# A feed-forward stage with TensorE's order from the program and its scale factors taken in three separated steps

## The chip, the cores and the metric

The kernel runs on one core of a Trainium2 chip (trn2). The metric is the device time of one execution in microseconds (us), given as the median of several runs. Beside the runs stands one execution recorded by the hardware profiler; all rows below come from it.

## The reference

Three layers follow one another: causal attention with a decay, a dense feed-forward layer with a low-rank token mixing, and a layer of four experts of causal attention with a gate that takes two of four. The change lies in the second, which is

```python
batch, seq, d_model = (4, 576, 512)
xt = x.transpose(0, 2, 1)
h = xt @ U @ V                       # rank 32
u = x + h.transpose(0, 2, 1)
ch = np.maximum(u @ w_ch1, 0.0) @ w_ch2      # 512 -> 2048 -> 512
return (u + ch).astype(np.float32)
```

The weights arrive as 64-bit words and are narrowed to 32 bits on the chip.

## The kernel before, in words

**Precision by two parts.** Every large product is made of three: high by high, high by low, low by high. For the first half of the hidden features the parts are fp32r; for the second half they are f16, and there weights and u are first multiplied by a power of two that brings their largest value into range.

**Tiling.** The hidden features are split into four quarters q of 512 (NQ = 4, FT = 4 tiles of 128). A batch of u is held as [128, 4, 576] in DRAM (udram) and worked on in two halves c of 288 columns (HC = 288, NC = 2). The sum y goes to ydram between visits.

**Steps.** The list `steps` (L529 to L541) has 32 entries (batch b, half c, quarter q): 0 to 15 do quarters 0 and 1 (fp32r), 16 to 23 quarters 2 and 3 of batches 0 and 1, 24 to 31 quarters 2 and 3 of batches 2 and 3 (f16). QX0 = 14, QX1 = 16 and QX2 = 24 are places in it. `ffn_stream` (L554) yields after each group: a group of 12 matmuls for a hidden tile of the *next* step (`ffn_hidden`, L497) alternates with a group of 12 for an output tile of this step (`ffn_out`, L513), eight groups a step. The hidden tile is evicted by ScalarE (hh, L508) and then VectorE (hl, L509), the output by VectorE (L523, or L525 with the scale taken back). Both kinds share three PSUM buffers (psf).

**Before and beside it.** Up to the last pair of attention heads the groups fill TensorE's gaps in the attention. 79 groups are done that way. The rest, from step 9 on, is the dense stage alone, and the changed lines are there.

**Weights of quarters 2 and 3.** `narrow_quarter` (L399) reads eight raw tiles of 512 KB on the SP queue into two buffers, narrows each on ScalarE (L338, L340) and VectorE (L341, L342) and takes its maximum on VectorE (L419). `power` (L381) makes a factor of 128 maxima: TensorE turns them into a row (amt, L384), VectorE takes the maximum and keeps the exponent bits (L388 to L390), TensorE spreads it over the partitions by a product with ones (rsp, L393), VectorE makes the factor and its reciprocal (es, L395 and L396). `convert_quarter` (L432) then writes the f16 parts on ScalarE (L447) and VectorE (L448) into the buffers that quarter 0 (pool wx) or quarter 1 (pool wy) leaves free. The loop at L933 does this for quarter 2 about QX0 and for quarter 3 about QX1, with one 8-tile buffer (wfull).

**u in f16.** `ffn_load16` (L451) loads a half of u on the SP queue (L456), takes its maximum (uam, L458), calls `power`, scales on ScalarE (uhf, L462) and VectorE (ulf, L463) and loads the sum (L465). It is called 12 times, from `ffn_prepare` two steps ahead: once per half and quarter for batches 0 and 1, once per half for batches 2 and 3. Its buffers are a pool of six (fy2) for steps 14 to 23, a pool of three (fy) else. The fp32r steps use `ffn_load` (L478) with a low part made by GpSimd (ul, L490).

**What sets the order.** Each engine has its own queue and works through it in order. Under `tc.manual_schedule(engines={PE})` TensorE's queue has the order of the program; the attention before and after runs like that. Elsewhere, and on all other engines and the SP queue always, a planner orders the instructions: it plays the program through with estimated durations and lets an engine take the earliest instruction of the program that is ready by these. Before the change the dense stage's TensorE order is the planner's too. After the stage `load_y` (L974) and the lines from L955 on bring in the experts' weights and the first y; the planner may start them during the stage.

Of the kernel before, what the change touches and what calls it, by code (L numbers as in the profile page):

```python
# [8 lines left out]
F32 = mybir.dt.float32  # L9
# [9 lines left out]
P = 128  # L19
# [42 lines left out]
def kernel(  # L62
# [318 lines left out]
    def power(am):  # L381
# [10 lines left out]
        rp = ps1.tile([P, 1], F32, name="rsp", tag="av")  # L392
# [6 lines left out]
    def narrow_quarter(w32, q):  # L399
# [15 lines left out]
        for t in range(2 * FT):  # L415
            if t + 1 < 2 * FT:
                read(t + 1)
            narrow_bytes(w32[:, t, :], raws.pop(0)[:].rearrange("p (n two) -> p n two", two=2))
            nc.vector.tensor_reduce(am[:, t // FT, t % FT:t % FT + 1], w32[:, t, :], AX.X, OP.max,  # L419
                                    apply_absolute_value=True)  # L420
            yield
        sides = []
        for s in range(2):
            a1 = cur["s16"].tile([P, 1], F32, name="wa1", bufs=2)
            nc.vector.tensor_reduce(a1[:], am[:, s, :], AX.X, OP.max)
            sides.append(power(a1[:]))
            yield
        back = cur["s16"].tile([P, 1], F32, name="wback", bufs=2)
# [3 lines left out]
    def convert_quarter(wp, w32, q):  # L432

        shapes = [[P, KT, FT * P]] * 2 + [[P, FT, DM]] * 2
        w1h, w1l, w2h, w2l = [wp.tile(sh, F16, name=n + "f", tag=n)
                              for sh, n in zip(shapes, ("w1h", "w1l", "w2h", "w2l"))]
        W[q] = w1h, w1l, w2h, w2l
# [13 lines left out]
    def ffn_load16(b, c, fy):  # L451

        fu = cur["fu"]
        cs = slice(c * HC, c * HC + HC)
        ust = fy.tile([P, KT, HC], F32, name="ust", tag="yc")
        nc.sync.dma_start(ust[:], udram[b, :, :, cs])  # L456
        am = cur["s16"].tile([P, 1], F32, name="uam", bufs=2)
        nc.vector.tensor_reduce(am[:], ust[:], AX.XY, OP.max, apply_absolute_value=True)  # L458
        es = power(am[:])
        uh = fu.tile([P, KT, HC], F16, name="uhf", tag="uh")  # L460
        ul = fu.tile([P, KT, HC], F16, name="ulf", tag="ul")
        nc.scalar.mul(uh[:], ust[:], es[:, 1:2])  # L462
        nc.vector.scalar_tensor_tensor(ul[:], ust[:], es[:, 1:2], uh[:], OP.mult, OP.subtract)  # L463
        yc = fy.tile([P, KT, HC], F32, name="yc", tag="yc")
        nc.sync.dma_start(yc[:], ydram[b, :, :, cs])  # L465
        return uh, ul, yc, es
# [30 lines left out]
    def ffn_hidden(t, weights, uh, ul, dt=F32R):  # L497
# [5 lines left out]
        for n, (wa, xa, k) in enumerate(todo):  # L503
            nc.tensor.matmul(ph[:], wa[:, k, fs], xa[:, k, :], start=n == 0,  # L504
# [39 lines left out]
    def ffn_prepare(i):  # L544
        if i >= len(steps) or i in loads:
            return
# [807 lines left out]
```

## Time and profile before

| what | value |
|---|---|
| time, median of 3 runs | 909.58 us (905.0 to 912.32) |
| the profiled execution's own time | 904.65 us |
| its span, first to last instruction | 902.9 us, mean granted TensorE clock 0.966 |
| TensorE matmuls busy | 796.7 us (88%), 7428 |
| VectorE busy | 615.9 us (68%) |
| ScalarE busy | 432.6 us (48%) |
| GpSimd busy | 282.8 us (31%) |
| DMA | 101.95 MB, 113 GB/s in the mean |

How to read the rows: PE is TensorE, PEld its weight loads, DVE VectorE, ACT ScalarE, POOL GpSimd, SP the engine whose queue issues most transfers; a q behind a name is that engine's sequencer. Times are us from the span's start. The chain is the work that ended last, followed back from the last instruction, each time to what released it. In a table of stretches a row has the stretch, its length, each engine's busy time with its instructions in brackets, the granted clock of TensorE (1.00 is 2.4 GHz, 0.50 is 1.2), the busy share of the 16 DMA engines and GB/s. A group of instructions has the line, engine, operation, out<-in, count, busy us, mean ns of one, and behind the last bar the engine's idle time just before them with what ended it. A row of the timeline has start, duration, engine, line, operation, and in brackets the idle time before it and its releaser. A wait has its sum in us, how often, and the longest. A matmul's end is modelled, so that neighbours overlap and a short gap doesn't show as idle time.

### The profile page before, as it was taken

To read this page: it belongs to the slowest core of one execution; us is meant where nothing else is said; L and a number is where in the kernel's file an instruction comes from. 1 tells how busy PE (TensorE), PEld (TensorE's weight loads), DVE (VectorE), ACT (ScalarE), POOL (GpSimd) and SP (SyncE) were. 2 spreads that over 40 slices of the span, in tenths; PEclk is the share of its full clock that TensorE was granted. 3 is DMA by queue.
4 is the path that set the end of the run, shared out by engine and by line. 5 is a ranking of instruction groups with operands and counts; after the bars stand their busy time and mean duration, and the time that the engine had idled before them with its cause. 6 is when DMAs were issued, how large, how long until landed. Compare 5 with 4: busy or idle time off the path is not lost.

```text
span 902.9 us, 19107 instructions
## 1 busy us (share of the span) xinstructions
PE 796.7 (88%) x7428; PEld 714.6 (79%) x7428; DVE 615.9 (68%) x1626; ACT 432.6 (48%) x836; POOL 282.8 (31%) x367
## 2 busy tenths in 40 slices
PE   2787587889999989989998798996999999989997
PEld 2686577879999889988986576774677889889886
DVE  6999898966766676547568755434443578876775
ACT  4686665654555544434235321223211367675664
POOL 9856546543423341031110000006100734341210
PEclk9998699999999999999998899998999999999999
DMA  6345475542432432035377434224310422412122
GB/s 189 111 115 157 135 231 160 177 151 81 127 102 76 120 102 75 15 114 176 110 258 221 133 106 131 80 80 132 103 53 28 125 55 66 107 47 75 34 74 86
DMA packets 67370, 101.95 MB, mean 113 GB/s; under 512 B 5152, under 2 KB 48016, under 8 KB 67280
## 3 DMA queue, kind: packets, MB, share of 16 engines
q1 hardware_dynamic: 62720, 91.96, 34.6%
q10 hardware_dynamic: 4560, 8.78, 2.6%
q8 instruction: 58, 0.95, 0.4%
q14 instruction: 32, 0.26, 0.1%
HBM read 60.33 MB, written 22.56 MB: 92 GB/s over the span
## 4 chain that ended last, share of the span: by engine, by line
PE 52%; DVE 19%; DMA 16%; ACT 5%; issue 4%; POOL 3%; SPq 1%; DVEq 0%; POOLq 0%; ACTq 0%
PE cps L520 15%; PE hps L504 13%; PE sc L228 6%; DMA ust<-udram 5%; DMA raw<-in_w_dram 5%; DVE ph L244 4%; PE po L1154 3%; PE pv L1112 2%; PE pq L1047 2%; DVE ub L185 2%; PE ub L180 2%; PE gp L710 2%; PE av L259 1%; PE av L263 1%; PE av L261 1%
## 5 line engine op out<-in xcount | busy, mean ns | idle before, releaser
L244 DVE TENSOR_TENSOR ph<-pf,ph 128x576 f16<-128x576 f32 x144 | 128.1, 894 | 30.4 <-ACT ph L243 29.6
L508 ACT ACTIVATE hh<-hps 128x288 fp32r<-128x288 f32 (+1 forms) x128 | 52.1, 409 | 185.9 <-PE hps L504 177.1
L509 DVE SCALAR_TENSOR_TENSOR hl<-hps,hh 128x288 fp32r<-128x288 f32 (+1 forms) x128 | 57.7, 451 | 77.2 <-ACT hh L508 76.5
L238 ACT ACTIVATE pf<-sc 128x576 f32<-128x576 f32 x144 | 84.4, 613 | 36.8 <-PE sc L228 29.9
L243 ACT CAST ph<-pf 128x576 f16<-128x576 f32 x144 | 89.6, 637 | 9.7 <-POOL pf L240 8.2
L228 PE MATMUL sc<-qa,ka 128*128 128x288 f32 (+4 forms) x288 | 74.0, 317 | 18.0 <-DMA qa<-mr 6.4
L185 DVE CUSTOM_DVE_ANT_0 ub<-ub,maskm 128x448 f32<-128x448 f32 x192 | 81.6, 425 | 10.7 <-PE ub L180 8.7
L520 PE MATMUL cps<-hh,w2h 128*128 128x288 f32 x256 | 81.2, 317 | 2.3 <-DVE hl L509 2.0
L520 PE MATMUL cps<-hh,w2hf 128*128 128x288 f16 x256 | 74.3, 290 | 5.2 <-DVE hl L509 4.4
L520 PE MATMUL cps<-hh,w2l 128*128 128x288 f32 x256 | 77.2, 302 | 0.0
L520 PE MATMUL cps<-hl,w2h 128*128 128x288 f32 x256 | 77.0, 301 | 0.0
L259 PE MATMUL av<-vh,ph 128*128 128x65 f16 x720 | 74.5, 199 | 2.0 <-DVE x L308 2.0
L504 PE MATMUL hps<-uh,w1h 128*128 128x288 f32 x256 | 74.0, 311 | 2.3 <-DVE hl L509 2.3
L504 PE MATMUL hps<-uhf,w1hf 128*128 128x288 f16 x256 | 68.7, 297 | 7.4 <-ACT uhf L462 6.2
L520 PE MATMUL cps<-hl,w2hf 128*128 128x288 f16 x256 | 74.3, 290 | 0.0
L520 PE MATMUL cps<-hh,w2lf 128*128 128x288 f16 x256 | 74.3, 290 | 0.0
L261 PE MATMUL av<-vl,ph 128*128 128x64 f16 x720 | 74.0, 196 | 0.0
L263 PE MATMUL av<-vh,ph 128*128 128x65 f16 x720 | 73.7, 196 | 0.0
L259 PEld LDWEIGHTS <-ph 128*128 128x128 f16 x720 | 67.6, 100 | 6.1 <-DVE x L308 2.1
L504 PE MATMUL hps<-uh,w1l 128*128 128x288 f32 x256 | 70.6, 298 | 0.0
L228 PEld LDWEIGHTS sc<-qa,ka 128*128 128x128 f32 x288 | 51.8, 198 | 23.6 <-ACT pf L238 5.0
L504 PE MATMUL hps<-uhf,w1lf 128*128 128x288 f16 x256 | 68.6, 296 | 0.0
(221 smaller groups left out, 2391.7 us busy)
## 6 DMA issues: line engine op xcount, KB each, us to landing
raw<-in_w_dram SPq DMA_DIRECT2D x32, 512.0 KB
ust<-udram SPq DMA_DIRECT2D x20, 576.0 KB
qkt<-in_qk_dram SPq DMA_DIRECT2D x16, 576.0 KB
yc<-ydram SPq DMA_DIRECT2D x14, 576.0 KB
ydram<-yc SPq DMA_DIRECT2D x14, 576.0 KB
vr<-in_v_dram SPq DMA_DIRECT2D x16, 320.0 KB
udram<-ustage ACTq DMA_DIRECT2D x16, 288.0 KB
ydram<-ust SPq DMA_DIRECT2D x8, 576.0 KB
```

Of the source, the lines that this page charges most:

```text
L185: nc.vector.tensor_tensor_reduce(ub[:, bk, off:off + w], ub[:, bk, off:off + w], maskm[:, S - w:S], 1.0, NEG, OP.add, OP.max, mx[:, t:t + 1])
L228: nc.tensor.matmul(ps[:, bk, off:off + w], wa, xa, start=bk not in banks[:n], stop=bk not in banks[n + 1:])
L238: nc.scalar.activation(pfv, view, AF.Exp, scale=ISC)
L243: nc.scalar.copy(ph[:, o0:o0 + n], pf[:, 0:n])
L244: nc.vector.tensor_tensor(pl[:, o0:o0 + n], pf[:, 0:n], ph[:, o0:o0 + n], OP.subtract)
L259: nc.tensor.matmul(av[:, it, :], ph[:, c:c + P], vh[:, jt, :], start=first, stop=False)
L261: nc.tensor.matmul(av[:, it, 0:64], ph[:, c:c + P], vl[:, jt, :], start=False, stop=False)
L263: nc.tensor.matmul(av[:, it, :], pl[:, c:c + P], vh[:, jt, :], start=False, stop=last)
L504: nc.tensor.matmul(ph[:], wa[:, k, fs], xa[:, k, :], start=n == 0, stop=n == 3 * KT - 1)
L508: nc.scalar.activation(hh[:], ph[:], AF.Relu)
L509: nc.vector.scalar_tensor_tensor(hl[:], ph[:], 0.0, hh[:] if dt == F16 else f32(hh[:]), OP.max, OP.subtract)
L520: nc.tensor.matmul(pc[:], wa[:, t, dsl], xa[:], start=n == 0, stop=n == 3 * FT - 1)
```

## The change

- `power` gives control back twice between the exponent bits and the product with ones, which moves to the PSUM banks of the scores (ps2).
- `narrow_quarter` gives control back twice a tile and four times at each factor. Both quarters have their own 8-tile buffer (wfull with 2) and are narrowed one after the other from the start of the dense stage.
- Quarters 2 and 3 share tiles of wx (`halves_of_weights`); wy's buffers take the sums of batches 2 and 3.
- `ffn_load16` is gone. `prepare_u` loads both halves of a batch, takes four maxima of [128, 2, 288] and one factor for the batch; `convert_u` loads the sums and converts in four pieces of 576 columns on each of the two engines. u's parts are [128, 4, 576] and serve both quarters; so do the sums.
- `ffn_prepare` serves fp32r steps alone, all from the pool of three (fy).
- The dense stage runs under `manual_schedule` for TensorE: after each group `dense_until` takes one piece from every job of a list. Steps 9 to 13: both quarters' narrowing, and u of batches 0 and 1. Step 14: conversion of quarter 2 and of u of batch 0. Step 15: u of batch 1. Step 16: conversion of quarter 3. From step 17 u of batch 2, from step 21 its conversion and u of batch 3, step 23 its conversion.

```diff
@@ power
-        rp = ps1.tile([P, 1], F32, name="rsp", tag="av")
+        yield
+        yield
+        rp = ps2.tile([P, 1], F32, name="rsp", tag="s2")
         nc.tensor.matmul(rp[:], every[:], full[:].bitcast(BF16)[:, 1:2], start=True, stop=True)
...
@@ narrow_quarter
             if t + 1 < 2 * FT:
                 read(t + 1)
+            yield
             narrow_bytes(w32[:, t, :], raws.pop(0)[:].rearrange("p (n two) -> p n two", two=2))
+            yield
             nc.vector.tensor_reduce(am[:, t // FT, t % FT:t % FT + 1], w32[:, t, :], AX.X, OP.max,
                                     apply_absolute_value=True)
-            yield
         sides = []
         for s in range(2):
             a1 = cur["s16"].tile([P, 1], F32, name="wa1", bufs=2)
             nc.vector.tensor_reduce(a1[:], am[:, s, :], AX.X, OP.max)
-            sides.append(power(a1[:]))
             yield
+            yield
+            sides.append((yield from power(a1[:])))
...
-    def ffn_load16(b, c, fy):
...
+    def prepare_u(b, fy):
+
+        us = []
+        for c in range(NC):
+            us.append(fy.tile([P, KT, HC], F32, name="ust", tag="yc"))
+            nc.sync.dma_start(us[c][:], udram[b, :, :, c * HC:c * HC + HC])
+        yield
+        yield
+        am = cur["s16"].tile([P, 2 * NC], F32, name="uam", bufs=2)
+        for n in range(2 * NC):
+            k = 2 * (n % 2)
+            nc.vector.tensor_reduce(am[:, n:n + 1], us[n // 2][:, k:k + 2], AX.XY, OP.max,
+                                    apply_absolute_value=True)
+            yield
+        a1 = cur["s16"].tile([P, 1], F32, name="ua1", bufs=2)
+        nc.vector.tensor_reduce(a1[:], am[:], AX.X, OP.max)
+        yield
+        yield
+        st_u[b] = us, (yield from power(a1[:]))
+
+    def convert_u(b, ycs):
+
+        us, es = st_u.pop(b)
+        uh = cur["fu"].tile([P, KT, S], F16, name="uhf", tag="uh")
+        ul = cur["fu"].tile([P, KT, S], F16, name="ulf", tag="ul")
+        for c, yc in enumerate(ycs):
+            cs = slice(c * HC, c * HC + HC)
+            nc.sync.dma_start(yc[:], ydram[b, :, :, cs])
+            for i, step in enumerate(steps):
+                if step[:2] == (b, c) and step[2] > 1:
+                    loads[i] = uh[:, :, cs], ul[:, :, cs], yc, es
+        for c in range(NC):
+            cs = slice(c * HC, c * HC + HC)
+            for k in range(0, KT, 2):
+                nc.scalar.mul(uh[:, k:k + 2, cs], us[c][:, k:k + 2], es[:, 1:2])
+                nc.vector.scalar_tensor_tensor(ul[:, k:k + 2, cs], us[c][:, k:k + 2], es[:, 1:2],
+                                               uh[:, k:k + 2, cs], OP.mult, OP.subtract)
+                yield
...
@@ ffn_prepare
-        if i >= len(steps) or i in loads:
+        if i >= QX1 or i in loads:
...
-            fy = cur["fy2"] if QX0 <= i < QX2 else cur["fy"]
-            loads[i] = ffn_load(b, c, first, fy) if q < 2 else ffn_load16(b, c, fy)
+            loads[i] = ffn_load(b, c, first, cur["fy"])
...
+    def dense_until(i):
+        while at[0] < i:
+            fill(1)
+            for job in list(jobs):
+                if next(job, 1):
+                    jobs.remove(job)
...
-    wfull = pool("wfull")
-    cur["fy2"] = pool("fy2", 6)
-    for q, wp, i0, i1 in ((2, wx_pool, QX0 - 2, QX0), (3, wy_pool, QX1 - 1, QX1)):
-        fill_until(i0)
-        w32 = wfull.tile([P, 2 * FT, DM], F32, name="w32")
-        behind.append(narrow_quarter(w32, q))
-        fill_until(i1)
-        more_weights(100)
-        behind.append(convert_quarter(wp, w32, q))
-        next(behind[0])
-    fill_until(QX2)
-    cur["fy2"].release()
+    wfull = pool("wfull", 2)
+    fy2 = pool("fy2", 6)
+    w32 = {q: wfull.tile([P, 2 * FT, DM], F32, name="w32") for q in (2, 3)}
...
+    with tc.manual_schedule(engines={mybir.EngineType.PE}):
+        jobs.append(in_turn(narrow_quarter(w32[2], 2), narrow_quarter(w32[3], 3)))
+        jobs.append(in_turn(prepare_u(0, fy2), prepare_u(1, fy2)))
+        dense_until(QX0)
+        halves_of_weights()
+        drain(jobs[1]) if len(jobs) > 1 else None
+        del jobs[1:]
+        quarters = [convert_quarter(w32[2], 2)]
+        jobs.append(convert_u(0, sums_of(fy2, ("yc", "yc"))))
+        while 2 not in scales:
+            next(jobs[0])
+        jobs.append(in_turn(*quarters))
+        dense_until(QX1 - 1)
+        jobs.append(convert_u(1, sums_of(fy2, ("yc", "yc"))))
+        dense_until(QX1)
+        drain(in_turn(*jobs))
+        del jobs[:]
+        jobs.append(convert_quarter(w32[3], 3))
+        dense_until(QX1 + 1)
+        jobs.append(prepare_u(2, cur["fy"]))
+        dense_until(QX1 + 5)
+        jobs.append(in_turn(convert_u(2, sums_of(wy_pool, ("w1h", "w1l"))),
+                            prepare_u(3, cur["fy"])))
+        dense_until(QX1 + 7)
+        drain(in_turn(*jobs))
+        del jobs[:]
+        jobs.append(convert_u(3, sums_of(wy_pool, ("w2h", "w2l"))))
+        dense_until(QX2)
+        drain(in_turn(*jobs))
+        del jobs[:]
+    fy2.release()
...
-    fill_until(len(steps))
+    with tc.manual_schedule(engines={mybir.EngineType.PE}):
+        dense_until(len(steps))
```

## Rows read from the trace of the kernel before

**Rows 1.** The page, the chain that ended last, shares by line.
```profile
PE cps L520 15%; PE hps L504 13%; PE sc L228 6%; DMA ust<-udram 5%; DMA raw<-in_w_dram 5%; DVE ph L244 4%; PE po L1154 3%; PE pv L1112 2%; PE pq L1047 2%; DVE ub L185 2%; PE ub L180 2%; PE gp L710 2%; PE av L259 1%; PE av L263 1%; PE av L261 1%
```
**Rows 2.** The dense stage in five stretches.
```profile
394.80:477.47 82.67, 75.37 (x549) 73.80 (x548) 50.70 (x108) 33.42 (x60) 10.72 (x4) 0.97 0.60 189
477.47:560.00 82.53, 72.69 (x525) 55.50 (x525) 57.43 (x130) 26.85 (x45) 0.00 (x0) 0.90 0.45 141
560.00:613.00 53.00, 53.00 (x437) 42.34 (x435) 20.79 (x48) 12.75 (x29) 4.55 (x9) 1.00 0.28 86
613.00:660.00 47.00, 37.40 (x282) 27.68 (x281) 21.09 (x48) 11.93 (x23) 13.35 (x14) 0.93 0.35 105
660.00:705.25 45.25, 45.25 (x372) 36.13 (x370) 16.03 (x35) 5.75 (x14) 0.00 (x0) 1.00 0.13 40
```
**Rows 3.** Stretches without a gap: nine fp32r groups, then 28 f16 groups.
```profile
442.45:456.79 14.34, 14.34 (x110) 14.34 (x109) 6.67 (x13) 4.97 (x9) 0.00 (x0) 1.00 0.50 164
571.42:612.58 41.16, 41.16 (x338) 32.88 (x336) 14.90 (x31) 9.96 (x24) 4.13 (x8) 1.00 0.30 93
```
**Rows 4.** The whole dense stage, TensorE alone: L504 (hidden), then L520 (output).
```profile
394.80:705.25 310.45, 149.12 (x1032) 113.87 (x1032) 0.96 0.40 124
394.80:705.25 310.45, 156.29 (x1092) 121.66 (x1092) 0.96 0.40 124
```
**Rows 5.** TensorE's waits from 394 to 706 us, two of them.
```profile
PE amt L384 <- DVE uam L458: 6.1, 5, 3.4
...
PE rsp L393 <- DVE ar L390: 4.6, 4, 2.1
```
**Rows 6.** The timeline of TensorE about 477 and 620 us.
```profile
477.47 0.40 PE L504 MATMUL hps<-uhf,w1hf 128*128 128x288 f16 x1 [2.60 <-ACT uhf L462]
...
619.83 0.37 PE L384 MATMUL amt<-ident,uam 128*1 128x128 f32 x1 [3.40 <-DVE uam L458]
```
**Rows 7.** VectorE from 394 to 706 us: groups of instructions, and one wait.
```profile
L509 DVE SCALAR_TENSOR_TENSOR hl<-hps,hh 128x288 f16<-128x288 f32 x64 | 28.9, 453 | 51.0 <-ACT hh L508 50.3
...
L458 DVE TENSOR_REDUCE uam<-ust 128x1 f32<-128x1152 f32 x12 | 16.1, 1350 | 18.9 <-DMA ust<-udram 18.9
...
L419 DVE TENSOR_REDUCE wam<-w 128x1 f32<-128x512 f32 x16 | 10.7, 676 | 0.1
...
DVE uam L458 <- DMA ust<-udram: 18.9, 10, 4.3
```
**Rows 8.** The timeline of the SP queue, 610 to 615 us.
```profile
610.57 1.03 SPq L958 DMA_DIRECT2D st<-in_wall_dram  x2
614.28 0.58 SPq L456 DMA_DIRECT2D ust<-udram  x1
```
**Rows 9.** Waits of ScalarE and VectorE from 394 to 706 us.
```profile
ACT w L338 <- DMA raw<-in_w_dram: 18.8, 7, 4.8
...
ACT wah L959 <- DMA st<-in_wall_dram: 7.5, 2, 5.6
...
DVE w L341 <- ACT raw L340: 6.2, 5, 3.1
```
**Rows 10.** The timeline of ScalarE at 408 us and TensorE at 413 us.
```profile
408.66 0.67 ACT L338 ACTIVATE w<-raw 128x512 int32<-128x512 uint8 x1 [3.69 <-DMA raw<-in_w_dram]
...
413.25 0.40 PE L520 MATMUL cps<-hh,w2h 128*128 128x288 f32 x1 [2.03 <-DVE hl L509]
```
**Rows 11.** The timeline of ScalarE at 455 us and TensorE at 461 us.
```profile
455.92 1.16 ACT L489 CAST uh<-ust 128x1152 fp32r<-128x1152 f32 x1 [1.64 <-DMA ust<-udram]
...
461.05 0.68 PE L504 MATMUL hps<-ul,w1h 128*128 128x288 f32 x4
```
**Rows 12.** The timeline of GpSimd and VectorE at 419 to 423 us.
```profile
419.26 2.69 POOL L490 TENSOR_TENSOR ul<-ust,uh 128x1152 fp32r<-128x1152 f32 x1 [12.78 <-ACT uh L489]
...
420.80 1.69 DVE L341 SCALAR_TENSOR_TENSOR w<-raw,w 128x512 int32<-128x512 int32 x1 [0.45 <-ACT raw L340]
422.53 0.69 DVE L342 SCALAR_TENSOR_TENSOR w<-raw,w 128x512 int32<-128x512 int32 x1
```

More of the change, by code (lines that the diff above doesn't have):

```diff
@@ L430, in narrow_quarter, with convert_quarter @@
         scales[q] = sides, back
[L432 to L437, printed above, removed]
+    def convert_quarter(w32, q):
+        w1h, w1l, w2h, w2l = W[q]
         sides = scales[q][0]
@@ L449, in convert_quarter @@
             yield
-    def ffn_load16(b, c, fy):
[L453 to L466, printed above, removed]
+    st_u = {}
@@ L503, in ffn_hidden @@
         for n, (wa, xa, k) in enumerate(todo):
-            nc.tensor.matmul(ph[:], wa[:, k, fs], xa[:, k, :], start=n == 0,
+            nc.tensor.matmul(ph[:], wa[:, k, fs], xa[:, k], start=n == 0,
                              stop=n == 3 * KT - 1)
@@ L921, in later_batches @@
         ffn_prepare(NPAIR - NP)
+    jobs = []
+    def dense_until(i):
[4 more added lines that the diff above has]
+                    jobs.remove(job)
     with tc.manual_schedule(engines={mybir.EngineType.PE}):
@@ new lines, with halves_of_weights, in_turn, sums_of @@
+    fy2 = pool("fy2", 6)
+    w32 = {q: wfull.tile([P, 2 * FT, DM], F32, name="w32") for q in (2, 3)}
+    def halves_of_weights():
+        shapes = [[P, 2, KT, FT * P]] * 2 + [[P, 2, FT, DM]] * 2
+        both = [wx_pool.tile(sh, F16, name=n + "f", tag=n)
+                for sh, n in zip(shapes, ("w1h", "w1l", "w2h", "w2l"))]
+        for q in (2, 3):
+            W[q] = [t_[:, q - 2] for t_ in both]
+    def in_turn(*gens):
+        for gen in gens:
+            yield from gen
+    def sums_of(p_, tags):
+        return [p_.tile([P, KT, HC], F32, name="yc", tag=n) for n in tags]
@@ new lines @@
+    more_weights(100)
+    with tc.manual_schedule(engines={mybir.EngineType.PE}):
[28 more added lines that the diff above has]
+        del jobs[:]
```

## The prediction

> **What bounds the kernel now.** I read the chain that ended last first. TensorE's two feed-forward lines lead it, but a tenth of the span stands there as two transfers, the load of u and of raw weights [rows 1]: TensorE is the engine that sets the end, and in places it waits for data. Next the stages. From 394.8 us, where the dense stage starts to run alone, to 705.25 us the table splits in two kinds [rows 2]: 560 to 613 and 660 to 705.25 are full (53.00 busy of 53.00, 45.25 of 45.25, granted clock 1.00), while the other three have 7.3, 9.8 and 9.6 us without a matmul and a granted clock of 0.97, 0.90 and 0.93, that is, they ran in part at 1.2 instead of 2.4 GHz. So the loss has places.
>
> How large is it? Where nothing is missing, nine groups of twelve fp32r matmuls take 14.34 us, 1.593 each, and 28 groups in f16 take 41.16 us, 1.470 each [rows 3]. The stretch holds (1032 + 1092) / 12 = 177 groups [rows 4]; the code makes 16 steps x 8 = 128 of them f16, which leaves 49. Packed they need 49 x 1.593 + 128 x 1.470 = 266.2 us. The stretch lasts 310.45, so **44.2 us** are lost, 26.7 of them as idle time and the rest as slow clock and as gaps that the modelled ends of matmuls cover.
>
> Who causes it? TensorE's waits name the factor: the turn waits for the maximum of u, the ones-product for VectorE's bits [rows 5]. Two holes show in order of time: 2.60 us before the first f16 product at 477.47, which waits for the converted u, and 3.40 before a turn at 619.83 [rows 6]. The last one is no arithmetic: VectorE's 12 maxima of u sat 18.9 us behind the load [rows 7], and that load was issued only at 614.28, behind loads of the next layer's weights on the same queue [rows 8].
>
> **The change part by part.** The sum is against the profiled execution, 904.65 us.
>
> Factors: u's go from 12 to 4, the weights' stay 4, so 16 turns and 16 ones-products become 8 each. In TensorE's queue maximum, turn and ones-product now stand two groups apart, 2 x 1.593 = 3.2 us for VectorE to answer, where its bits were waited for 4.6 us in four places, 1.15 each [rows 5]. That takes the waits of [rows 5] away where VectorE is less than 3.2 us behind.
>
> u: 12 loads of 576 KB become 8, and four reloads of the sum y go too, since steps q=2 and q=3 of batches 0 and 1 now share one sum (its store after q=2 remains, unread). All but the last two f16 batches are loaded right after 394.8, the others after step 17, ahead of the next layer's weights on the SP queue: the hole at 619.83 should close. VectorE's maximum: 512 columns take 0.676 us, 1152 take 1.350 [rows 7]; a line through both gives 0.744 for 576. So 12 x 1.350 = 16.2 become 16 x 0.744 = 11.9, and the scaled copy and its low part of u are made 8 times instead of 12. All that is off TensorE's path.
>
> Conversion: the first f16 product needed the factor, u and the weights in one chain. Now the weights of quarter 2 and u of batch 0 are converted behind the eight groups of step 14, one step (12.7 us) ahead. This ends the hole of 472 to 477.
>
> Costed at nothing: both quarters in one tile of the old wx buffers and the last sums in those of wy (same bytes, free by then: quarter 1's last product is in step 15, the sums come at step 21), and the ones-product in the scores' PSUM banks, which nothing else uses in this stage. If they were not free, the conversion would wait as before and the hole of 472 to 477 stay, some 5 us.
>
> What comes back, each term with both bounds:
> - Raw weights. Quarter 3's narrowing moves up beside quarter 2's. ScalarE sat 18.8 us behind raw loads in 7 of 16 tiles [rows 9], in order, with the hidden layer's eviction behind it: it stood 3.69 us before 408.66 and TensorE lost 2.03 at 413.25 [rows 10], then ran at half clock for a while. I count 4 us for a quarter in the first window: two quarters 8 (0, if a tile every second group is slow enough for the loads, to 18.8). The queues give no more room: some five 512 KB reads and four 576 KB loads more are 4.9 MB in 75 us, 65 GB/s on top of 189 that took 0.60 of the DMA engines [rows 2], so 0.8 of them.
> - Steps 14 and 15 load fp32r u into the pool of three buffers instead of the pool of six, behind the store of an older sum. Before, ScalarE waited for such a load to 455.92, and the four products with its low part were put behind another group, to 461.05 [rows 11]. With a fixed order nothing passes: 2 us (0 to 5).
> - VectorE against GpSimd. At 420.80 an operation took 1.69 us where the next, of the same shape, took 0.69: it ended 0.54 us behind GpSimd's 2.69 us subtraction from 419.26 [rows 12]. Four such subtractions stand in the stretch; at 1.0 each 4 us of VectorE at most, 1.5 taken, 0 below.
> - VectorE's maxima behind late loads of u: 18.9 us for 10 of 12, 1.9 each [rows 7]. Three PSUM buffers give two groups, 2.9 us, less two evictions (VectorE's is 0.453 [rows 7], ScalarE's taken alike): about 2.0 of cover. So 1.5 us in all (0, to 8 x 1.9 = 15 with the cover gone).
> - The eight turns and ones-products themselves: 1 us (0, to 8 x 0.4 = 3 if each pair costs about what the turn at 619.83 takes, 0.37 [rows 6]).
> - ScalarE's 7.5 us behind the next layer's weights, longest 5.6 [rows 9], still ahead of evictions: 3 (0 to 7.5).
>
> Sum 17.0, so the gain is 44.2 - 17.0 = 27.2 and the execution 877.4. The median of the three runs lies 4.9 above the profiled one; part of that scatter is waiting for transfers, so I add 1.5: **879**.
>
> The Trainium skill, page "SBUF — State Buffer", section "Who interferes with whom", says that a Vector instruction with two SBUF inputs and a GpSimd instruction that reads SBUF lock one another out, the second blocked until the first ends. The trace agrees at 420.80. By that rule every one of the new Vector operations is exposed to the four subtractions, 4 us instead of the 1.5 taken, and the time would be 881.5.
>
> **The rivals.**
> *Nearly all of it comes.* Slower narrowing (one tile in two groups) lets the loads land; only the factor's own products, u's lateness and a wait for the next layer's weights remain, some 5 us: 865. For it: 660 to 705.25 is perfectly full at 16.03 us of VectorE [rows 2]. Against: raw loads and u's loads now share the first 60 us. Chance 0.15.
>
> *VectorE becomes the bound up to step 15.* In program order the 37 groups to step 14 carry 14.5 tiles x 2.06 = 29.9 (0.69 twice [rows 12] and 0.676), evictions 37 x 0.45 = 16.7, maxima 8 x 0.744 = 6.0, factors 4 x 1.15 = 4.6: 57.2 us of VectorE in 59 us of TensorE. If it also sits through 6.2 us behind raw weights [rows 9] and 4 x 1.9 behind u, the stretch grows by 12; the rest of the tiles and the conversions in step 14 add some 3; GpSimd 4; the slow clock after such waits some 4; other terms 7. That is 30 lost and 14 gained: 904.65 - 14 + 1.5 = 892. For it: VectorE is busy for 50.70 of 82.67 us there already [rows 2], before most of quarter 3's tiles and u's maxima arrive. Against: quarter 3 isn't needed before step 19, so what is left of it may stand behind the evictions. Chance 0.21.
>
> *The loss only moves: no change.* Only TensorE's order is fixed; ScalarE's, VectorE's and SP's still come from the planner's estimates. If loads are as late as before against its estimates, all terms stand at their upper ends, 18.8 + 5 + 4 + 15 + 3 + 7.5 = 53: 904.65 + 53 - 44.2 = 913.5, with the 1.5 some 915. Chance 0.10.
>
> *Slower.* One mechanism: the fixed queue. Eight factors make 16 places where TensorE, with ready groups behind it, stands for VectorE. Each costs VectorE's lag less 3.2 us. With the other terms at 17, 44.2 is used up at 1.7 each, a lag of 4.9 us; at a lag of 6 the places cost 45 and the time is 904.65 + 45 - 27.2 = 922. Against: the longest wait for a maximum was 3.4 without any distance [rows 5]. Chance 0.06.
>
> **How the numbers follow.** Forecast 0.48 (868 to 889), then 0.15, 0.21, 0.10, 0.06. The range 861 to 899 leaves out the last two cases (0.16) and the outer edges of the second and third, some 0.2 in all. A measurement of this kernel can tell about 1% from no change, 9 us: faster 0.84 (the first three), same 0.10, slower 0.06.
>
> **What would show it.** Right: no wait of TensorE above 1 us behind a maximum or factor, no idle hole before the first f16 product, granted clock 1.00 from step 16 on, 8 turns, and the stretch of 177 groups near 283 us. The raw term is right if ScalarE still waits 10 to 19 us for raw weights and TensorE's remaining gaps lie before step 14. Wrong: VectorE above 90% busy from 395 to 470 with TensorE waiting for low parts (third case); turns that still wait (slower); waits for u's low part at steps 13 to 15 above 5 us; or gaps outside the dense stage, which I take as unchanged.

## The result and the profile after

| | before | after |
|---|---|---|
| median | 909.75 us (19 runs) | 898.17 us (19 runs) |
| ratio | | 0.987 [0.9844, 0.9896] |
| profiled execution: time, span | 904.65, 902.9 us | 901.39, 899.7 us |
| dense stage alone, first to last product | 310.5 us | 296.6 us |

Faster, by 11.6 us (1.3%), where some 30 were forecast; 898 lies just inside the upper edge of the range. The stage was to shrink from 310.5 to 283.2 us and came to 296.6: half of its gain is missing. Some executions ran in a slower state, some per cent longer; ratios and intervals, here and below, leave these out, and the one that was profiled for repaired_late (889.78 us; the median of its undisturbed ones is 883.0) was such a one.

The chain of after by lines (answers [rows 1]): the two transfers went from 5% each to 4% and 3%.
```profile
PE cps L545 15%; PE hps L529 14%; PE sc L228 6%; DVE ph L244 4%; DMA ust<-udram 4%; DMA raw<-in_w_dram 3%; PE po L1227 3%; PE pv L1185 3%; DVE ub L185 2%; PE pq L1120 2%; PE ub L180 2%; DMA ydram<-ust 2%; PE gp L734 2%; PE av L259 1%; PE av L263 1%
```
The stage in five stretches (answers [rows 2], same columns; the first ends at the first f16 product). In this execution it starts at 402.2 us.
```profile
402.20:492.37 90.17, 77.31 (x552) 75.02 (x550) 67.54 (x146) 43.35 (x76) 11.02 (x4) 0.96 0.59 182
492.37:560.00 67.63, 63.61 (x491) 51.30 (x491) 31.05 (x73) 13.22 (x28) 0.00 (x0) 0.95 0.26 83
560.00:613.00 53.00, 53.00 (x434) 42.22 (x433) 25.15 (x57) 16.10 (x36) 0.98 (x4) 1.00 0.29 90
613.00:656.00 43.00, 39.56 (x321) 31.19 (x320) 13.72 (x31) 8.74 (x21) 21.64 (x33) 1.00 0.18 54
656.00:698.80 42.80, 42.80 (x352) 34.20 (x350) 14.71 (x32) 5.34 (x13) 0.00 (x0) 1.00 0.09 29
```
The later half is nearly repaired: 3.4 us idle in 613 to 656, clock 1.00. The front half isn't: 12.9 us idle before the first f16 product, 4.0 behind it, the clock below 1.00 in both.

TensorE's waits from 402 to 525 us (answers [rows 5]), then waits of ScalarE and VectorE in the stage (answers [rows 9] and the last row of [rows 7]): sum, times, longest.
```profile
PE rsp L395 <- DVE ar L390: 6.2, 2, 3.5
PE cps L545 <- DVE hl L534: 4.3, 2, 4.0
PE amt L384 <- DVE ar L388: 2.6, 1, 2.6
PE hps L529 <- POOL ul L515: 1.4, 1, 1.4
PE hps L529 <- ACT uh L514: 0.9, 1, 0.9
PE cps L545 <- DVE ust L548: 0.9, 1, 0.9
```
```profile
ACT w L338 <- DMA raw<-in_w_dram: 19.8, 11, 4.1
DVE uam L465 <- DMA ust<-udram: 10.5, 3, 6.0
DVE w L341 <- ACT raw L340: 7.7, 7, 2.9
ACT wah L1031 <- DMA st<-in_wall_dram: 12.9, 4, 5.4
```
So the factor's products still wait, but in three of their sixteen places (before, in nine waits [rows 5]). The timeline of TensorE at those places and at the worst eviction, then of VectorE, ScalarE and the SP queue just before them:
```profile
436.11 0.27 PE L384 MATMUL amt<-ident,ua 128*1 128x128 f32 x1 [2.59 <-DVE ar L388]
449.64 0.16 PE L395 MATMUL rsp<-ar,every 128*128 128x1 bf16 x1 [3.48 <-DVE ar L390]
492.37 0.16 PE L395 MATMUL rsp<-ar,every 128*128 128x1 bf16 x1 [2.75 <-DVE ar L390]
521.01 0.40 PE L545 MATMUL cps<-hh,w2hf 128*128 128x288 f16 x1 [3.99 <-DVE hl L534]
521.20 0.44 PE L545 MATMUL cps<-hh,w2lf 128*128 128x288 f16 x1
521.44 0.44 PE L545 MATMUL cps<-hl,w2hf 128*128 128x288 f16 x1
```
```profile
435.78 0.27 DVE L388 TENSOR_REDUCE ar<-amt 1x1 f32<-1x128 f32 x1
447.11 0.66 ACT L338 ACTIVATE w<-raw 128x512 int32<-128x512 uint8 x1 [4.12 <-DMA raw<-in_w_dram]
448.48 0.69 DVE L341 SCALAR_TENSOR_TENSOR w<-raw,w 128x512 int32<-128x512 int32 x1 [2.89 <-ACT raw L340]
483.39 0.62 SPq L459 DMA_DIRECT2D ust<-udram  x1
488.78 1.41 DVE L465 TENSOR_REDUCE uam<-ust 128x1 f32<-128x576 f32 x2 [3.10 <-DMA ust<-udram]
496.10 0.53 SPq L459 DMA_DIRECT2D ust<-udram  x1
514.86 0.52 SPq L459 DMA_DIRECT2D ust<-udram  x1
519.18 1.41 DVE L465 TENSOR_REDUCE uam<-ust 128x1 f32<-128x576 f32 x2 [6.01 <-DMA ust<-udram]
520.51 0.45 DVE L534 SCALAR_TENSOR_TENSOR hl<-hps,hh 128x288 f16<-128x288 f32 x1
```
What is to be seen. **492 and 521:** VectorE stands 3.10 and 6.01 us at a maximum of u of batch 2 or 3, whose load was issued 5.4 and 4.3 us earlier; behind it in its queue stand, the first time, two conversions of u and the bits of another factor (a weights' factor of quarter 3), the second time an eviction. Nothing needs these maxima yet, u of batch 3 least of all. Afterwards products follow each other every 0.24 us where 0.12 is usual: the granted clock is 0.50, 1.2 GHz, from 493.3 to 496.7 and from 520.6 to 524.0. **450:** the raw tile is late for ScalarE (4.12), then VectorE stands at L341 (2.89) with the factor's bits behind it. **436:** the turn of u's maxima waits for VectorE to have read *another* factor's row: quarter 2's weights and u of batches 0 and 1 (it is 1's turn that waits) have two independent jobs, and both write their row into the one PSUM buffer of tag "av"; VectorE reads the other row only at 435.78.

### The profile page after: what moved, and what is told of

It is laid out like the page before. It is cut to its first block, busy times and chain, and to the rows that moved or that the text cites. A ratio compares the mean times of both kernels' runs of the same rounds, so it can differ in the third digit from the quotient of the medians.

```text
span 899.7 us, 19048 instructions
## 1 busy us (share of the span) xinstructions
PE 795.6 (88%) x7412; PEld 720.2 (80%) x7412; DVE 608.0 (68%) x1598; ACT 428.8 (48%) x840; POOL 282.8 (31%) x367
## 4 chain that ended last, share of the span: by engine, by line
PE 54%; DVE 19%; DMA 14%; ACT 5%; issue 4%; POOL 3%; SPq 1%; POOLq 0%; ACTq 0%; DVEq 0%
PE cps L545 15%; PE hps L529 14%; PE sc L228 6%; DVE ph L244 4%; DMA ust<-udram 4%; DMA raw<-in_w_dram 3%; PE po L1227 3%; PE pv L1185 3%; DVE ub L185 2%; PE pq L1120 2%; PE ub L180 2%; DMA ydram<-ust 2%; PE gp L734 2%; PE av L259 1%; PE av L263 1%
## 5 line engine op out<-in xcount | busy, mean ns | idle before, releaser
L243 ACT CAST ph<-pf 128x576 f16<-128x576 f32 x144 | 89.7, 638 | 10.1 <-POOL pf L240 8.7
L228 PE MATMUL sc<-qa,ka 128*128 128x288 f32 (+4 forms) x288 | 75.8, 324 | 18.5 <-DMA qa<-mr 6.9
L529 PE MATMUL hps<-uh,w1h 128*128 128x288 f32 x256 | 76.3, 319 | 3.7 <-DVE hl L534 2.8
L228 PEld LDWEIGHTS sc<-qa,ka 128*128 128x128 f32 x288 | 53.8, 207 | 23.8 <-ACT pf L238 5.5
L259 PEld LDWEIGHTS <-ph 128*128 128x128 f16 x720 | 67.7, 100 | 6.1 <-DVE x L308 2.1
L261 PEld LDWEIGHTS <-ph 128*128 128x128 f16 x720 | 68.2, 101 | 0.0
L263 PEld LDWEIGHTS <-ph 128*128 128x128 f16 x720 | 68.1, 100 | 0.0
```

Source lines behind the costliest of these rows:

```text
L228: nc.tensor.matmul(ps[:, bk, off:off + w], wa, xa, start=bk not in banks[:n], stop=bk not in banks[n + 1:])
L243: nc.scalar.copy(ph[:, o0:o0 + n], pf[:, 0:n])
L259: nc.tensor.matmul(av[:, it, :], ph[:, c:c + P], vh[:, jt, :], start=first, stop=False)
L261: nc.tensor.matmul(av[:, it, 0:64], ph[:, c:c + P], vl[:, jt, :], start=False, stop=False)
L263: nc.tensor.matmul(av[:, it, :], pl[:, c:c + P], vh[:, jt, :], start=False, stop=last)
L529: nc.tensor.matmul(ph[:], wa[:, k, fs], xa[:, k], start=n == 0, stop=n == 3 * KT - 1)
```

## Experiments

All concern the dense stage, so beside the ratio each run is read by its stretch. Packed, it would take 266.2 us [rows 3, 4]; what it takes beyond is lost, split at the first f16 product and 40 f16 groups later (each part less its fp32r groups x 1.593 and f16 groups x 1.470). A stretch is that of one profiled execution: where no edit reaches, the parts repeat well (the rest is 3.8 to 4.4 us in eight of the runs), but one or two us in a whole stretch are not told from chance, and the ratios' intervals tell about 1% at best.

| kernel | ratio to before [95%] | stretch | lost | before f16 | first 40 | rest |
|---|---|---|---|---|---|---|
| before | 1 | 310.5 | 44.3 | 11.0 | 19.8 | 13.5 |
| after | 0.987 [0.9844, 0.9896] | 296.6 | 30.4 | 18.5 | 7.6 | 4.2 |
| pe_planner | 0.9839 [0.9758, 0.9919] | 296.5 | 30.3 | 16.0 | 10.1 | 4.2 |
| no_weight_max | 0.983 [0.9748, 0.9911] | 292.5 | 26.3 | 16.6 | 5.9 | 3.8 |
| raw_kept | 0.995 [0.9917, 0.9983] | 303.2 | 36.9 | 15.9 | 16.6 | 4.4 |
| u_max_kept | 0.9863 [0.9781, 0.9945] | 297.1 | 30.9 | 25.7 | 1.1 | 4.0 |
| raw_deep | 0.9953 [0.9922, 0.9984] | 303.5 | 37.2 | 30.2 | 6.7 | 0.3 |
| q3_late | 0.9781 [0.9697, 0.9866] | 287.8 | 21.6 | 6.5 | 11.1 | 4.0 |
| combo | 0.9888 [0.9857, 0.992] | 295.5 | 29.3 | 22.4 | 6.6 | 0.3 |
| u23_alone | 0.9733 [0.9686, 0.978] | 289.7 | 23.5 | 18.0 | 1.1 | 4.3 |
| amt_alone | 0.9822 [0.9759, 0.9885] | 294.7 | 28.4 | 15.1 | 9.3 | 4.0 |
| fy2_alone | 0.9773 [0.9731, 0.9815] | 286.4 | 20.2 | 15.2 | 4.2 | 0.8 |
| u23_amt_fy | **0.9687 [0.9656, 0.9717]** | 279.4 | 13.2 | 11.2 | 1.2 | 0.9 |
| repaired_late | 0.9662 [0.9607, 0.9716] | 278.4 | 12.2 | 4.5 | 6.6 | 1.1 |

**Is TensorE's fixed order the gain, or the loss?** pe_planner gives the order back to the planner and keeps all else:
```diff
-    with tc.manual_schedule(engines={mybir.EngineType.PE}):
+    if True:
```


> The changed kernel with TensorE's order in the dense stage left to the planner again; jobs, factors and loads as changed. If the fixed order is what brought the gain, the time goes back by most of it, to about 1.00 of the kernel before and a dense stretch near 310 us. If earlier loads, fewer factors and the distance between a factor's parts brought it, it stays within 0.5% of the changed kernel (0.987) and the dense stretch within 3 us of its 296.5. I expect the first by half: 0.993.

The stretch is the same to 0.1 us (its first two parts differ by 2.5 us, one each way), and the ratios' intervals overlap: half of the gain was expected to go, and none went. No gain or loss by TensorE's order itself is to be seen; what came must have come from fewer factors, early loads and earlier conversion, which no run tells apart.

**Is VectorE the bound?** no_weight_max leaves out the sixteen maxima of the weights (the factor comes from a constant), 16 x 0.676 = 10.8 us of VectorE.
```diff
-            nc.vector.tensor_reduce(am[:, t // FT, t % FT:t % FT + 1], w32[:, t, :], AX.X, OP.max, ...)
+        nc.gpsimd.memset(am[:], 0.15)
```


> The changed kernel without the 16 maxima over narrowed weight tiles on VectorE (a constant stands in their place, so the weights' factors are fixed ones): 10.8 us of VectorE's work gone, all in steps 9 to 15, and nothing else. VectorE too busy: the stretch up to step 15 shrinks by 8 us or more, 0.977 of the kernel before. Late transfers: 3 us at most, 0.984.

From its start to the first f16 product, and VectorE's two waits:
```profile
398.50:486.80 88.30, 77.64 (x552) 75.10 (x551) 58.72 (x127) 43.49 (x76) 10.99 (x4) 0.96 0.59 183
...
DVE uam L464 <- DMA ust<-udram: 9.5, 4, 4.9
DVE w L341 <- ACT raw L340: 13.2, 11, 3.6
```
VectorE is busy for 58.72 us in place of 67.54, and 1.9 us come back before the first f16 product, 4.1 in all. Much of what was taken away turned into waiting: 13.2 us at L341 in place of 7.7. The 8 us or more that a bound would have given back did not come: the amount of VectorE's work is not the bound; what its queue stands at is.

**Which late data?** Two orders pinned to the program's place, where the planner had been free to move them: raw_kept pins the first narrowing operation of ScalarE, u_max_kept the maxima of u.
```diff
@@ narrow_bytes  (raw_kept)
-        nc.scalar.activation(wi, raw.bitcast(U8)[:, :, 3], AF.Copy, ...)
+        tc.keep_in_program_order(nc.scalar.activation(wi, raw.bitcast(U8)[:, :, 3], AF.Copy, ...))
@@ prepare_u  (u_max_kept)
-            nc.vector.tensor_reduce(am[:, n:n + 1], us[n // 2][:, k:k + 2], AX.XY, OP.max, ...)
+            tc.keep_in_program_order(nc.vector.tensor_reduce(am[:, n:n + 1], ...))
```


> The changed kernel with the first narrowing operation of each raw tile pinned to its place in the program on ScalarE. Late transfers: the 3.48 us that TensorE waits before a ones-product at 449.6 and the half clock behind it go, 6 us less, 0.980 of the kernel before; ScalarE's 19.8 us behind raw loads fall below 10. VectorE too busy: no change, 0.987.

> The changed kernel with the maxima of u pinned to their place in the program on VectorE, so that the planner can't put them in front of evictions while the load is still under way. Theory 'late transfers in queues that work in order': TensorE's waits of 2.75 us at 492 and 3.99 us at 521 and the half clock behind them go, 9 us less, 0.977 of the kernel before. Rival 'VectorE has too much to do up to step 15': the same work stays, 2 us less at most, 0.985.

raw_kept did remove the wait before the ones-product of 450, and ScalarE's waits for raw tiles fell from 19.8 to 14.8 us (below 10 was expected), but the stretch lost 6.5 us more: the narrowing moved back, and the last factor with it (a turn waits 6.37 us at 500.28, where after had none). u_max_kept did remove both waits at 492 and 521 (first 40 groups: 7.6 to 1.1), so these were the maxima's; but it lost 7.2 more before the first f16 product, and the time stayed where it was (0.9863; 0.977 was expected). The timeline of TensorE, VectorE and GpSimd there:
```profile
415.86 0.37 PE L384 MATMUL amt<-ident,ua 128*1 128x128 f32 x1 [7.21 <-DVE ua L470]
...
405.88 2.78 DVE L342 SCALAR_TENSOR_TENSOR w<-raw,w 128x512 int32<-128x512 int32 x1
...
405.44 2.67 POOL L516 TENSOR_TENSOR ul<-ust,uh 128x1152 fp32r<-128x1152 f32 x1 [33.65 <-ACT uh L515]
```
Pinned, the maxima of batches 0 and 1 fall among the planner's narrowing operations, one of them 2.78 us long beside GpSimd, and TensorE's turn stands. Pinning is right for the batches whose data come late, wrong for those whose data are there.

**More buffers for raw weights?** raw_deep reads three tiles ahead into four buffers of its own.
```diff
-            raw = stage.tile([P, 2 * DM], I32, name="raw", tag="wraw")
+            raw = cur["raws"].tile([P, 2 * DM], I32, name="raw", tag="wraw")
...
-        read(0)
+        for t in range(3):
+            read(t)
```


> The changed kernel with four buffers for raw weight tiles in place of two, read three tiles ahead. If the late raw loads are the cause of what is lost before the first f16 product (18.5 us beyond packed groups in the changed kernel), ScalarE's 19.8 us behind them fall below 8, that loss falls to about 10 and the dense stretch from 296.6 to 288. If VectorE's amount of work is the cause, the tiles come sooner and bunch: the loss stays above 16.

It got worse. Three stretches of 10 us, then VectorE and GpSimd at 421 and TensorE behind them:
```profile
420.00:430.00 10.00, 5.64 (x36) 5.19 (x36) 10.00 (x12) 3.67 (x6) 5.89 (x2) 0.92 0.34 102
430.00:440.00 10.00, 8.43 (x58) 8.12 (x56) 9.83 (x21) 5.95 (x10) 0.00 (x0) 0.91 0.69 215
440.00:450.00 10.00, 4.49 (x30) 4.27 (x31) 9.76 (x26) 5.69 (x9) 0.00 (x0) 0.94 0.76 214
```
```profile
421.32 2.73 DVE L341 SCALAR_TENSOR_TENSOR w<-raw,w 128x512 int32<-128x512 int32 x1
423.98 3.12 DVE L342 SCALAR_TENSOR_TENSOR w<-raw,w 128x512 int32<-128x512 int32 x1
...
420.66 5.89 POOL L516 TENSOR_TENSOR ul<-ust,uh 128x1152 fp32r<-128x1152 f32 x2 [41.62 <-ACT uh L515]
...
428.71 0.61 PE L546 MATMUL cps<-hh,w2h 128*128 128x288 f32 x1 [4.36 <-DVE hl L535]
```
Now VectorE is full for 30 us: with tiles at hand the planner packs narrowing ahead of evictions and bits. And two operations that take 0.68 elsewhere take 2.73 and 3.12 while GpSimd makes two subtractions; TensorE stood 4.36 us behind the eviction that came next. ScalarE's wait for raw data fell only from 19.8 to 17.1 us.

**Quarter 3 later.** q3_late narrows quarter 3 from step 15 on, not beside quarter 2 (its first operation pinned); its conversion and u of batch 2 follow two steps later.
```diff
-        jobs.append(in_turn(narrow_quarter(w32[2], 2), narrow_quarter(w32[3], 3)))
+        jobs.append(narrow_quarter(w32[2], 2))
...
-        dense_until(QX1)
+        jobs.append(narrow_quarter(w32[3], 3))
+        dense_until(QX1 + 2)
```


> The changed kernel with one part undone: quarter 3 is narrowed from step 15 on, held there on ScalarE, and converted in step 18. If narrowing it beside quarter 2 is what costs before the first f16 product (by VectorE's work or by its loads), the loss there falls from 18.5 us to the 11 of the kernel before, and little comes back behind it, where VectorE has room: dense stretch 290. If the loss there comes from the fp32r loads of u and from the factors, it stays within 3 us of 18.5.

12.0 us less before the first f16 product (7.5 were expected), 3.5 more behind it: with its other waits in place, the kernel is 8.8 us shorter this way. The run moves three things together (narrowing, conversion and u of batch 2) and does not say which one counts.

**Repairs together.** combo has raw_deep's buffers with two repairs: maxima pinned for batches 2 and 3 only, and u's turn in a PSUM buffer of the scores. u23_amt_fy leaves the raw reads as they are and has these two and a third: u of steps 14 and 15 goes into the pool of the f16 sums (8 buffers, not 6), so that the pool of three is free.
```diff
@@ prepare_u  (u23)
+            if b > 1:
+                tc.keep_in_program_order(ins)
@@ power  (amt)
-        at_ = ps1.tile([1, P], F32, name="amt", tag="av")
+        at_ = (ps2.tile([1, P], F32, name="amt", tag="s2") if apart else ps1.tile(...))
@@ ffn_prepare  (fy2)
-            loads[i] = ffn_load(b, c, first, cur["fy"])
+            loads[i] = ffn_load(b, c, first, cur["fy2" if i >= QX0 else "fy"])
```


> Four raw buffers, pinned maxima of batches 2 and 3 and a second PSUM buffer for u's turn together; u of steps 14 and 15 as in the changed kernel. If these causes add up: 8 + 6.5 + 2.6 us less than the changed kernel, dense stretch 280, 0.970 of the kernel before. If VectorE takes their place before the first f16 product: 289, 0.979.

> The changed kernel with three small repairs: the maxima of u of batches 2 and 3 pinned to their place on VectorE, the turn for u in another PSUM buffer than the turn for weights, and the u of steps 14 and 15 in the larger pool (eight buffers). Late transfers and held buffers as the cause: the 7.6 us lost in the first 40 f16 groups become 1, the 2.6 us of the turn go, the 4 to 5 us of steps 14 and 15 go: dense stretch 283, 0.972 of the kernel before. VectorE too busy: the part before the first f16 product keeps its 18.5 us and the stretch is 290.

combo's stretch, 295.5, is neither of the two that were expected. Before the first f16 product it loses 22.4 us, less than raw_deep and more than after: the bunching is still there. In the first 40 groups it loses 6.6 like raw_deep, though no maximum waits for a load there any more: the planner has put the next layer's weights into these groups, ScalarE stands 4.01 and 5.09 us behind them (at 518.40 and 524.73) with evictions behind it, and TensorE 3.22 at 526.50. u23_amt_fy runs in 881.25 us (median): about the gain that was forecast for the change, and its stretch is 3.6 us shorter than the 283 that were expected. In the trace, start to first f16 product, to 560, and the rest:
```profile
396.90:479.80 82.90, 76.72 (x552) 74.32 (x551) 68.28 (x143) 41.89 (x74) 10.64 (x4) 0.98 0.66 208
479.80:560.00 80.20, 79.50 (x646) 64.36 (x646) 40.26 (x92) 19.67 (x42) 0.00 (x0) 1.00 0.32 104
560.00:676.40 116.40, 115.99 (x949) 92.36 (x947) 46.06 (x102) 24.93 (x60) 22.66 (x36) 1.00 0.18 56
```
From the first f16 product on TensorE is now all but full at 2.4 GHz, with the same VectorE work before it (68.28 us).

**Each repair alone.**

> The kernel after, with one edit: the maxima of u of batches 2 and 3 (only these) are pinned to their place in program order on VectorE. Theory (VectorE's queue stands behind maxima that the planner put too early, for loads that land later than it reckons): the waits of the ones-product before 492.4 and of the product before 521.0 go, with the half clock behind them, the loss of the first 40 f16 groups falls from 7.6 to about 1, what is lost before 477 stays at 18 to 19, the stretch goes to about 289, ratio 0.978. Rival (VectorE is short of time, so that the maxima are paid for at a later place): the loss of the first 40 f16 groups stays above 4 or that of the rest rises from 4.2 to above 7, ratio 0.984 or more.

> The kernel after, with one edit: the turn of the maxima of u stands in a PSUM buffer of the scores (tag s2) and no longer in the one buffer of tag av that the weights' factor uses as well. Theory (each of three waits costs what its place on TensorE's timeline shows, and they are independent): the 2.6 us wait of the turn before 436.1 goes and nothing else does, the loss beyond packed groups falls from 30.4 to about 28, the dense stretch from 296.6 to about 294, ratio to the kernel before 0.984. Rival (the waits are one chain, so that the first one removed moves the next): the stretch stays at 296 to 298, ratio 0.987. Other rival (the turn was what held the ones-product of 449.6 too): some 6 us less, ratio 0.980.

> The kernel after, with one edit: u of steps 14 and 15 is loaded into the pool of the f16 sums, made 8 buffers in place of 6, and not into the pool of three. Theory (the loss of some 5 us at step 15 is the wait for a buffer to come free, hence a late load): the load of step 15 is issued some 10 us earlier, TensorE's waits between 470 and 480 (0.94, 1.40, 0.92) go, the loss before the first f16 product falls from 18.5 to 13 or 14, the stretch to about 292, ratio 0.981. Rival (the load is late because it stands behind raw reads on SP's queue, whatever its buffer): the waits stay within 1 us and the stretch at 295 to 297, ratio 0.987.

u23_alone: 6.9 us off the stretch, 6.5 of them in the first 40 groups, as expected. Its ratio is clear of that of after. amt_alone: 1.9, too little for one profile or for the ratio to tell. The turn's wait is gone, and the one before the ones-product of 450 with it; 3.4 us come back before the first f16 product, but other waits have come in (1.66 at 446.74, 3.17 at 483.38, again behind a maximum), and 1.7 go in the first 40 groups. So the waits are not independent, and 1.9 is a balance, not the price of one wait. fy2_alone: 10.2, twice what was expected, and for the most part for other reasons. Its SP queue with one wait of VectorE and one of ScalarE, then the SP queue of after:
```profile
447.10 0.52 SPq L459 DMA_DIRECT2D ust<-udram  x1
...
461.74 0.52 SPq L519 DMA_DIRECT2D yc<-ydram  x1
462.31 0.63 SPq L509 DMA_DIRECT2D ust<-udram  x1
462.98 0.63 SPq L459 DMA_DIRECT2D ust<-udram  x1
...
SPq L519 <- DMA ydram<-ust: 6.6, 2, 3.8
...
DVE uam L465 <- DMA ust<-udram: 6.8, 5, 3.2
ACT wah L1031 <- DMA st<-in_wall_dram: 6.6, 4, 2.6
```
```profile
464.18 0.52 SPq L519 DMA_DIRECT2D yc<-ydram  x1
464.75 0.62 SPq L509 DMA_DIRECT2D ust<-udram  x1
...
SPq L519 <- DMA ydram<-ust: 7.2, 2, 3.6
```
Step 15's load (L509) is issued 61.6 us into the stage against 62.6: unchanged, since on SP it stands behind the reading back of a sum that waits for its store to land (L519). Of the three waits of TensorE that were to go, the 0.94 went; the 1.40 for u's low part and the 0.92 stayed. So the expected reason failed for the most part, and so did the rival's (raw reads). Of the 10.2, 3.3 come back before the first f16 product, where other waits stand than in after; no one cause of these is shown. The rest is later. With the pool of three free, batch 2's two loads go out 46 and 62 us into the stage and no longer 81 and 94: VectorE's waits at maxima fall from 10.5 to 6.8 us, the longest from 6.0 to 3.2, and the first 40 groups lose 3.4 us less. And ScalarE's waits for the next layer's weights fall from 12.9 to 6.6 us, the longest from 5.4 to 2.6, and the rest of the stretch loses 3.4 us less; why those loads meet ScalarE better is not shown. So u23 and fy2 repair one fault, the maxima, from two sides, and that is where their sum is too large: the three alone sum to 19.0 us and together give 17.2, and the 1.8 between them lie in the first 40 groups (6.5 - 1.7 + 3.4 = 8.2 alone, 6.4 together).

> The kernel after with the three repairs together (u of batches 2 and 3 pinned, its own PSUM buffer for u's turn, u of steps 14 and 15 in the pool of 8) and quarter 3 narrowed after quarter 2's conversion, from step 18 on, in place of beside quarter 2. Theory (the narrowing of quarter 3 in the first 80 us is a cost of its own, 12 us in the run with only that edit, and adds to the three): of the 13.2 us that the three repairs leave, 11.2 of them before the first f16 product, some 6 go, the stretch comes to about 273 and the ratio to about 0.962. Rival (with the repairs made, the raw reads of the first 80 us are no longer on TensorE's path, or narrowing quarter 3 later collides with maxima and conversions of batches 2 and 3): the stretch stays at 278 to 285, ratio 0.968 or above.

In this run quarter 3 is narrowed from step 15 on, as in q3_late; step 18 is that of its conversion. The rival held: added to the repairs, the late quarter 3 gains 6.7 us before the first f16 product and loses 5.6 behind it (a product waits 2.42 us at 506.35 for its eviction, which stands in VectorE's queue behind a narrowing operation that waited 3.44 for ScalarE); the stretch is 278.4 against 279.4 and the intervals overlap. With the other waits gone, no difference by where quarter 3 is narrowed is to be told.

## Why the prediction came out half right

The sum's own terms, with what the stretch of after lost (44.3 before, 30.4 now, 17.0 forecast). A us at 1.2 GHz counts half; 6.8 us of it stand about the wait of 450, 3.4 behind each of the other two. The split is read from the timeline of one execution, its last row is what remains, and since the waits are not independent it says where the time went, not what the removal of one wait would bring.

| term | forecast | measured |
|---|---|---|
| raw weights | 8 (0 to 18.8) | 3.48 at 450, 0.5 at 425, 3.4 for the slow clock: 7.4 |
| u of steps 14 and 15 | 2 (0 to 5) | 0.94 + 1.40 = 2.3 |
| **maxima behind late loads of u** | **1.5 (0 to 15)** | **2.75 + 3.99 + 3.4 for the slow clock = 10.1** |
| two turns in one PSUM buffer | not foreseen | 2.6 |
| next layer's weights | 3 (0 to 7.5) | 1.47 + 0.82 + 1.15 = 3.4 |
| eight pairs, VectorE against GpSimd, the rest | 1 + 1.5 | 0.92 at 477 (GpSimd), the rest 3.7: 4.6 |

**The step that failed** is the fourth term: "18.9 us for 10 of 12, 1.9 each", against "about 2.0 of cover". It divided a sum of waits by their count, though the same row gave 4.3 as the longest [rows 7]; the cover takes from each wait separately, so only the long ones count. After the change VectorE stands 10.5 us in three waits, and the two long ones reach TensorE: 6.01 becomes 3.99, so the cover of 2.0 was right; of the 3.10, with two conversions of 0.80 us in between, 2.75 arrive. The slow clock behind them, 3.4 us more, was not in this term. So it is 8.6 of the 13.4 us by which the loss exceeds the sum. It also priced all batches alike, though it had batches 2 and 3 loaded later than the others: the planner sends batch 2's loads out 81 and 94 us into the stage, from a pool of three that steps 14 and 15 still hold, and puts the maxima right behind them, ahead of bits and evictions that TensorE waits for. "All that is off TensorE's path" was wrong for these. u23_alone shows it: pinning eight maxima removes both waits and brings 6.9 us net of 10.1 (6.8 us of slow clock came in elsewhere, from 477).

**The second fault**, small, is in "costed at nothing": the ones-product's new banks were looked at, the turn's old buffer, now used by two jobs at once, was not. It is 2.6 us on the timeline; the 1.9 of amt_alone are a balance of several waits and no price of it.

**What held.** The size of the loss before and its places; 8 turns for 16; the wait for a maximum at 619.83 gone; the raw term in size (7.4 for 8, though amt_alone and fy2_alone lose the wait at 450 without an edit to the raw tiles; ScalarE waits 19.8 us for raw data, forecast 10 to 19); the next layer's weights (3.4 for 3, though ScalarE's waits for them grew from 7.5 to 12.9 us). Of the signs named beforehand 8 turns was right; wrong were the stretch near 283, TensorE's gaps all before step 14 (492 and 521 are behind it), "no wait above 1 us behind a maximum or factor" (2.59, 3.48, 2.75), "no idle hole before the first f16 product" (2.75), and the clock at 1.00 from step 16 on (only from some 525 us).

**The rivals.** "Nearly all of it comes" (865) fell: 30.4 us are still lost. The time, 898, is near the 892 of "VectorE becomes the bound up to step 15", but not by its mechanism: VectorE is 75% busy there (67.54 of 90.17), not above 90%, and 10.8 us of work less brought 1.9 there. "Only moves" fell (13.9 us of the stretch did come). "Slower by fixed queue" fell: 3 of its 16 places cost anything, and the planner's order is no better (pe_planner). That 898 is still inside the range is no credit to the sum, which gave 879: the range reached far into the second rival.

**VectorE against GpSimd** was taken at 1.0 a subtraction. In after it cost 3.35 us for two operations at 473.32 where the next two took 1.53; of that at most the 0.92 before an output product at 477.10 reached TensorE. raw_deep shows the far end: 2.73 and 3.12 for 0.68 each, and 4.36 us of TensorE. There both operations end 0.55 us behind a subtraction, as the one at 420.80 did before the change. The rule cited in the prediction from the Trainium skill, page "SBUF — State Buffer", section "Who interferes with whom" (the second is blocked until the first ends), describes these rows better than the mean that was taken. The Trainium skill, page "PSUM — Partial Sum Buffer", section "Engine vs sequencer instructions", says that VectorE's queue is strictly first in, first out; the rows at 488.78 and 519.18 agree: what stood behind the waiting maximum (3.10 and 6.01 us) came after it. That is the mechanism of the failed term.

**Outside the stage.** The stretch fell by 13.9 us, the profiled spans by 3.2, the medians by 11.6. Ahead of the stage the order of the compute engines is unchanged, yet it starts at 402.2 in place of 394.8; over the thirteen profiles of after and the experiments the start lies between 394.1 and 403.4, so this is scatter. Behind it, up to the kernel's last product, after takes 196.9 us, before 193.7, the experiments 194.3 to 202.3. There is one profile of before, so whether some 3 us are lost there to the change stays open. That the planner hoists the maxima because it reckons the loads shorter than they are is argued from the issue and landing times, not shown. Not tried: step 15's load ahead of the sum's reading back on SP (up to 2.3 us).

## What to carry to other kernels

A wait of an engine that is not the bound costs by its longest instance against the cover behind it, not by its mean; ask for every instruction with a transfer behind it what stands next in its queue. Work for later steps is harmless only where its data are there: pin it to its place in the program where they come late, and leave it free where they are early. An edit that removes one wait also moves others, so price it by the stretch and not by the wait. Where two jobs of the same kind start to run side by side, count the single buffers that they share, PSUM too, and the loads that share a small pool.

## What was not expected of the hardware

- Waits of 2.75 and 3.99 us of TensorE were each followed by products at 1.2 GHz (0.24 us from one to the next, not 0.12), some 1.7 us each on top of the wait; the stretch had 27.3 us at this clock before, 13.7 after, 3.4 in u23_amt_fy. In repaired_late a wait of 2.42 us was followed by none.
- More room for loads made the stage slower, by the order that the planner made of it: four raw buffers cost 6.9 us of stretch, though ScalarE's wait for raw data fell by 2.7.
- A VectorE operation beside GpSimd's subtraction can take four times its time (0.68 to 2.73 and 3.12).
